# Values unit of an attention kernel: query tiles outside, the two key tiles inside

## The chip, the cores and the metric

One core of a Trainium2 chip runs the kernel. The metric is the device time of one execution in microseconds (us). The executions of each kernel agree within 0.2%, with a granted TensorE clock of 0.999 or 1.0. The clock is the one granted to TensorE, the matrix engine, as a share of full speed.

## The reference, cut to what matters

The reference normalises `x` (2048 rows of 640), runs attention with 32 heads of width 192 over caches of 2048 keys, multiplies the result by a gated feed-forward branch and adds `x`. The change touches one product only, the probabilities times the values:

```python
H, Dh = 32, 192
scores = jnp.einsum("bhqd,bhkd->bhqk", q, k_cache) * (Dh ** -0.5)
p = _softmax(scores, axis=-1)
o = jnp.einsum("bhqk,bhkd->bhqd", p, v_cache)          # this product
return o.transpose(0, 2, 1, 3).reshape(B, Sq, H * Dh) @ wo
```

## The kernel before

For each head, each block of 512 queries and each pair `p` of key tiles (two tiles of 128 keys), TensorE computes scores into PSUM (the memory that takes its results), ScalarE takes the exponential into `pT2` (128 keys on the partitions; columns 0 to 511 are the 512 queries for key tile 0, columns 512 to 1023 for key tile 1), and TensorE multiplies `pT2` with V. That last part is the *values unit*. There are 32 heads x 4 query blocks x 8 pairs = 1024 units.

V lies in `vt`: 16 rows (one per key tile) of 192 values, a column of ones for the softmax sum, and one column of padding, so 194 bf16 numbers or 388 bytes a row.

```python
vts = [vtp.tile([P, NKT, DH + 2], BF16, name=f"vt{i}") for i in range(2)]
# ... cut: loads of K, V and weights, LayerNorm, projections ...
def emit_scores(h, qb, p):
    # ... cut: operands
    for r, (ka, qa, kb, qb2) in enumerate(rounds):          # 3 rounds of 2 row halves, 512 columns
        nc.tensor.matmul(st2[:, 0:512], lhsT=ka, rhs=qa, start=r == 0 and nr == 3, stop=r == nr - 1)
        nc.tensor.matmul(st2[:, 512:1024], lhsT=kb, rhs=qb2, start=r == 0 and nr == 3, stop=r == nr - 1)
    pT2 = pp.tile([P, 1024], BF16, tag="pT2", name="pT2")
    nc.scalar.activation(out=pT2[:], in_=st2[:], func=ACT.Exp, scale=att_scale)
    return pT2

def values(n):
    # ... cut: PSUM tiles obanks[0], obanks[1] at p == 0
    vt = loads[h]["vt"]
    pT2 = exps.pop(n)
    for t in range(2):                                      # key tile
        for j in range(4):                                  # query tile
            start = p == 0 and t == 0 and j % 2 == 0
            stop = p == NPAIR - 1 and t == 1 and j % 2 == 1
            for r in range(2):                              # row half of the array
                nc.tensor.matmul(obanks[r][:, j * 256:j * 256 + DH + 1],
                                 lhsT=pT2[r * 64:(r + 1) * 64, t * 512 + j * P:t * 512 + (j + 1) * P],
                                 rhs=vt[r * 64:(r + 1) * 64, 2 * p + t, 0:DH + 1], start=start, stop=stop)
    # ... cut: after the last pair VectorE adds the two halves and divides by the sums
```

The stationary operand (`lhsT`) is a 64 x 128 piece of `pT2`; the moving operand (`rhs`) is half of a V row tile, 64 partitions by 193 columns. The two matmuls of the inner loop use the two row halves of the array and run side by side (in the trace of before the second starts 3 ns after the first, in the median); I call them a *pair of matmuls*, so a unit is eight pairs in a row.

## Time and profile before

| | before |
|---|---|
| time, median of 6 runs | 1941.95 us (1940.68 to 1942.10) |
| PE busy in the profiled run | 1929.6 of 1938.7 us |
| share of values matmuls in the chain of waits | 35% |
| PE waiting for other engines | 3.5 us in all |

The first view is the page of the profiled run: span, busy time of each engine, the chain of waits by engine and by line, then groups of instructions (line, engine, operation, output<-inputs, shapes, count | busy us, mean ns of one | idle time of the engine before them).

```profile
span 1938.7 us, 59672 instructions
...
PE 1929.6 (100%) x27273; PEld 1318.5 (68%) x27281; DVE 654.0 (34%) x997; ACT 1180.2 (61%) x1278; POOL 282.6 (15%) x501
...
PE 98%; DVE 1%; DMA 0%; ACT 0%; issue 0%; POOL 0%; DVEq 0%; ACTq 0%
PE obank L516 35%; PE st L487 33%; PE ps L424 14%; PE ps_s L111 11%; PE ps_f L727 3%; PE ps_gu L701 1%; PE st L488 1%; DVE stats L316 0%; PE ps L410 0%; DMA x_all<-in_A_x_dram 0%; DVE xn L346 0%; PE ps L391 0%; PE pst L354 0%; DVE mv L317 0%; PE pk L271 0%
...
L516 PEld LDWEIGHTS <-pT 64*128 64x128 bf16 x16384 | 713.7, 94 | 242.2 <-ACT pT L490 0.2
L516 PE MATMUL obank<-vt,pT 64*128 64x193 bf16 x16384 | 851.8, 243 | 0.0
L487 PE MATMUL st<-qC,KW 64*128 64x512 bf16 x2046 | 605.6, 376 | 0.1
...
```

PE, the matmul engine, is never out of work, and 98% of the chain is PE. The Trainium skill, "Trainium Kernel Development and Optimization", section "Performance Expectations", calls matmul busy time a bad metric for how close a kernel is to roofline, because matmuls are pipelined. The trace agrees that busy time hides the pace: 16384 values matmuls of 243 ns would be 3981 us; they are busy for 851.8 us together because they overlap. So the spacing of their starts has to be read, not their length.

The second view lists what PE waited for (us in total, times, longest).

```profile
...
engine line waited for: us in total, times, longest us
PE pk L569 <- POOL ident_bf masks.py:199: 2.8, 1, 2.8
PE st L487 <- ACT pT L490: 0.3, 1, 0.3
PE pst L354 <- DVE xn L346: 0.2, 1, 0.2
PE st L483 <- DVE qA L393: 0.2, 1, 0.2
```

After the start nothing makes PE wait. The third view follows V's tile: the instructions that read or write it (shortest, median and longest ns, first and last start in us), and who waited for it.

```profile
...
engine op xcount: duration ns min/median/max, first and last start us, forms
L516 PE MATMUL obank<-vt,pT x16384: 241/243/253, 16.0 to 1646.4; 64*128 64x193 bf16 x200
...
  DVE osum L525: 788.9, 127
...
DMA to landing us min/median/max: 3.6/5.6/7.5
```

The last values matmul starts at 1646.4 us; the remaining 292 us are the other stages.

From the start times of the single matmuls in the trace I worked out the distance from the start of each pair of matmuls to the next, averaged over the units of the trace that are complete and hold no wait (1016 of 1024; a unit with a distance over 120 ns is left out). The last column is the time of the three pairs of scores just ahead of a unit, averaged over all 1022 such stretches:

```
           pair:   1     2     3     4     5     6     7     8    unit  | 3 pairs of scores
before           83.3  83.3  83.3  83.3  87.5  82.5  82.5  82.8  668.6 | 647.5 ns
```

The fifth pair stands out. It is the one at which the moving operand goes from the even V row (key tile 0) to the odd one (key tile 1).

One more line, of the view of groups kept apart by shape: 48 full-array matmuls that accumulate onto one PSUM address back to back.

```profile
...
L111 PE MATMUL ps_s<-wo_sb,oT 128*128 128x128 bf16 x48 | 2.8, 219 | 0.0
...
```

### The profile page before, as it was taken

How to read it: one execution, taken by the hardware profiler on the slowest of the kernel's cores; microseconds unless marked ns; L12 is line 12 of the kernel's file. 1: busy time of each engine (PE TensorE's matmuls, PEld its weight loads, DVE VectorE, ACT ScalarE, POOL GpSimd, SP SyncE). 2: the span in 40 equal slices, each digit the busy share in tenths (PEclk: the TensorE clock that was granted, in tenths of full speed). 3: DMA queues.
4: the chain of work that ended last, by engine and by line, in shares of the span. 5: the costliest groups of instructions: out<-in, count | busy, mean ns of one | idle time of the engine just before them, and what ended most of it. 6: DMA issues, size and time to landing. Idle time of an engine off the chain costs nothing.

```text
span 1938.7 us, 59672 instructions
## 1 busy us (share of the span) xinstructions
PE 1929.6 (100%) x27273; PEld 1318.5 (68%) x27281; DVE 654.0 (34%) x997; ACT 1180.2 (61%) x1278; POOL 282.6 (15%) x501
## 2 busy tenths in 40 slices
PE   9999999999999999999999999999999999999998
PEld 6666666666666666666666666666666666577776
DVE  7333333333333333333333333333333334521111
ACT  6677676767676767776767777677767677210000
POOL 3111111111111111111111111111111110000000
PEclk9999999999999999999999999999999999999999
DMA  7643433323233433353434333434333220937772
GB/s 181 129 101 67 98 68 86 83 60 88 59 89 62 99 62 98 68 162 68 101 65 100 68 101 68 101 64 100 69 71 94 57 69 2 262 67 135 152 152 61
DMA packets 394643, 178.98 MB, mean 92 GB/s; under 512 B 341616, under 2 KB 382832, under 8 KB 394384
## 3 DMA queue, kind: packets, MB, share of 16 engines
q1 hardware_dynamic: 371136, 125.32, 30.3%
q0 software_dynamic: 19472, 45.71, 9.6%
q8 instruction: 215, 3.52, 0.8%
q10 hardware_dynamic: 3776, 4.06, 0.6%
q14 instruction: 44, 0.36, 0.1%
HBM read 52.82 MB, written 27.79 MB: 42 GB/s over the span
## 4 chain that ended last, share of the span: by engine, by line
PE 98%; DVE 1%; DMA 0%; ACT 0%; issue 0%; POOL 0%; DVEq 0%; ACTq 0%
PE obank L516 35%; PE st L487 33%; PE ps L424 14%; PE ps_s L111 11%; PE ps_f L727 3%; PE ps_gu L701 1%; PE st L488 1%; DVE stats L316 0%; PE ps L410 0%; DMA x_all<-in_A_x_dram 0%; DVE xn L346 0%; PE ps L391 0%; PE pst L354 0%; DVE mv L317 0%; PE pk L271 0%
## 5 line engine op out<-in xcount | busy, mean ns | idle before, releaser
L490 ACT ACTIVATE pT<-st 128x1024 bf16<-128x1024 f32 x1024 | 1046.2, 1022 | 251.8 <-PE st L488 236.2
L516 PEld LDWEIGHTS <-pT 64*128 64x128 bf16 x16384 | 713.7, 94 | 242.2 <-ACT pT L490 0.2
L516 PE MATMUL obank<-vt,pT 64*128 64x193 bf16 x16384 | 851.8, 243 | 0.0
L487 PE MATMUL st<-qC,KW 64*128 64x512 bf16 x2046 | 605.6, 376 | 0.1
L525 DVE COPY osum<-obank 128x772 f32<-128x772 f32 x128 | 123.0, 961 | 788.9 <-PE obank L516 788.9
L488 PE MATMUL st<-qB,KW 64*128 64x512 bf16 x1024 | 385.0, 376 | 0.0
L487 PE MATMUL st<-qA,KW 64*128 64x512 bf16 x1022 | 384.3, 376 | 0.4 <-ACT pT L490 0.3
L488 PE MATMUL st<-qC,KW 64*128 64x512 bf16 x1022 | 384.3, 376 | 0.0
L488 PE MATMUL st<-qA,KW 64*128 64x512 bf16 x1022 | 384.3, 376 | 0.0
L487 PEld LDWEIGHTS <-KW 64*128 64x128 bf16 x3068 | 278.0, 94 | 153.8 <-issue 2.1
L424 PE MATMUL ps<-xnT,W 64*128 64x512 bf16 x1280 | 297.2, 376 | 0.0
L424 PE MATMUL ps<-xnS,W 64*128 64x512 bf16 x1280 | 296.3, 376 | 0.0
L488 PEld LDWEIGHTS <-KW 64*128 64x128 bf16 x3068 | 278.0, 94 | 0.7 <-issue 0.6
L377 POOL DMA_DIRECT2D qC<-qA x124 | 65.4, 528 | 1285.6 <-DVE rl_all L532 1270.0
L430 ACT CAST qB<-ps 128x512 bf16<-128x512 f32 x131 | 76.7, 586 | 228.5 <-PE ps L424 222.9
L111 PE MATMUL ps_s<-wo_sb,oT 128*128 128x384 bf16 (+3 forms) x1535 | 208.8, 299 | 0.1
L424 PEld LDWEIGHTS <-W 64*128 64x128 bf16 x2560 | 122.9, 94 | 121.2
L111 PEld LDWEIGHTS <-oT 128*128 128x128 bf16 x1536 | 148.4, 98 | 60.4
L526 DVE TENSOR_TENSOR osum<-osum,obank 128x772 f32<-128x772 f32 x128 | 122.7, 958 | 13.4
L533 DVE TENSOR_TENSOR ostage<-osum,rl_all 128x768 bf16<-128x768 f32 x128 | 122.6, 958 | 4.4
L465 DVE SCALAR_TENSOR_TENSOR hT<-pt,qB 64x512 bf16<-64x512 bf16 x64 | 43.8, 684 | 199.5 <-ACT pt L464 199.5
L429 DVE CAST qA<-ps 128x512 bf16<-128x512 f32 x131 | 90.5, 691 | 25.2 <-PE ps L410 7.3
(84 smaller groups left out, 623.8 us busy)
## 6 DMA issues: line engine op xcount, KB each, us to landing
o_scr<-ostage SPq DMA_DIRECT2D x16, 1536.0 KB, 10.0
vt<-in_A_v_cache_dram SPq DMA_DIRECT2D x63, 384.0 KB, 5.6
qC<-qA POOLq DMA_DIRECT2D x248, 64.0 KB, 1.9
qC<-qB POOLq DMA_DIRECT2D x124, 64.0 KB, 2.3
wo_sb<-in_A_wo_dram POOLq DMA_DIRECT2D x1, 7680.0 KB, 35.3
W<-in_A_wq_dram POOLq DMA_DIRECT2D x32, 160.0 KB, 3.4
W<-in_B_w_dram POOLq DMA_DIRECT2D x32, 80.0 KB, 3.1
W<-in_A_wq_dram POOLq DMA_DIRECT2D x32, 80.0 KB, 2.9
```

The lines of the kernel that those rows point to most:

```text
L111: nc.tensor.matmul(ps[:, 0:w], lhsT=oT[:, k, :], rhs=wo_sb[:, k, c0:c1], start=(k == 0), stop=(k == OC - 1))
L377: nc.gpsimd.dma_start(out=qC[0:64, half, :], in_=qAB[half][64:P, :])
L424: nc.tensor.matmul(ps[:, r * 512:(r + 1) * 512], lhsT=W[rows, j, :], rhs=xs[rows, j // 2, qs], start=(j == 0), stop=(j == 2 * DC - 1))
L429: a = nc.vector.tensor_copy(out=qAB[0][:], in_=ps[:, 0:512])
L430: b = nc.scalar.copy(out=qAB[1][:], in_=ps[:, 512:1024])
L487: nc.tensor.matmul(st2[:, 0:512], lhsT=ka, rhs=qa, start=r == 0 and nr == 3, stop=r == nr - 1)
L488: nc.tensor.matmul(st2[:, 512:1024], lhsT=kb, rhs=qb2, start=r == 0 and nr == 3, stop=r == nr - 1)
L490: nc.scalar.activation(out=pT2[:], in_=st2[:], func=ACT.Exp, scale=att_scale)
L516: nc.tensor.matmul(obanks[r][:, j * 256:j * 256 + DH + 1], lhsT=pT2[r * 64:(r + 1) * 64, t * 512 + j * P:t * 512 + (j + 1) * P], rhs=vt[r ...
L525: nc.vector.tensor_copy(out=osum[:], in_=ov[0])
L526: nc.vector.tensor_tensor(out=osum[:], in0=osum[:], in1=ov[1], op=ALU.add)
L533: nc.vector.tensor_tensor(out=ostage[:, qb * 4:qb * 4 + 4, hg * DH:(hg + 1) * DH], in0=osum[:, :, 0:DH], in1=rl.unsqueeze(2).to_broadcast( ...
```

## The change

The intent was to finish one query tile (both key tiles) before going to the next. The same 16 matmuls run, in another order.

```diff
         pT2 = exps.pop(n)
-        for t in range(2):
-            for j in range(4):
+        for j in range(4):
+            for t in range(2):
                 start = p == 0 and t == 0 and j % 2 == 0
                 stop = p == NPAIR - 1 and t == 1 and j % 2 == 1
                 for r in range(2):
```

The accumulation stays right: each `start` flag is still on the first matmul into its half of the tile, and e2, which has the same order, passed the comparison with the reference.

## The prediction

> **What bounds it.** TensorE. The page gives PE busy for 1929.6 of 1938.7 us at a granted clock of 0.99 or more, the chain of waits is 98% PE, and in the table of waits PE waits for other engines for 3.5 us in all. So any time the change adds to or takes from TensorE's stream is the change in the kernel's time; ACT (61%) and DVE (34%) have slack.
>
> **What the values unit costs.** The values matmuls are 35% of the chain: 1024 units of 16 matmuls, run as 8 pairs (both row halves of the array at once). From the trace's start times, averaged over 1021 complete units, a unit takes 669.5 ns; its pairs' start-to-start times are 83.3, 83.3, 83.3, 83.3, 87.5, 82.5, 82.5, 82.8 ns. The Trainium skill, "TensorE: Matmul & The Clock Gate", section "Back-to-back issue gap", gives N/2.4 + 2.5, so 82.9 ns for 193 columns: the trace agrees but for the fifth pair, which costs 4.6 ns more in every unit.
>
> **What the change does.** It permutes the 16 matmuls of a unit. Count, shapes, weight loads, PSUM groups and the other engines' instruction order stay. What moves:
> 1. Each PSUM address is written again one pair (83 ns) after its first write, not four pairs (333 ns).
> 2. The V operand changes row at each pair; before, once, at the fifth pair.
> 3. In the first unit of each head the wait for V's second half comes at the third matmul instead of the ninth, 0.25 us sooner. V was loaded a head earlier: no cost.
>
> **Costing.** (1) I expect 0: in the last output tile 48 matmuls of 128 columns accumulate onto one address back to back, 56 ns apart, at the normal rate. (2) is where the fifth pair matters. Rows of V are 194 bf16 = 388 bytes, so even rows start at a multiple of 8 bytes and odd rows 4 bytes off. Scores and projections change their moving operand at each pair too, between well-aligned tiles, and show no extra (215.8 ns for 512 columns). So I read the fifth pair as the cost of going from an aligned to a misaligned row. (The Trainium skill, "SBUF — State Buffer", Specifications, speaks of lines of 16 bytes; no run here shows that as the mechanism.) Going back seems free: the scores after a unit start on time. After the change a unit has four such steps instead of one: three more at 5 ns, 15 ns per unit, x 1024 = 15 us, all on the critical path. If going back costs the same, six more: 28 us (1970). If the fifth pair's extra comes from something else (returning to the first PSUM bank, say), it may vanish (1938) or stay (1942).
>
> **Prediction.** 1955 us, 0.7% slower; 8 in 10 within 1938 to 1970. Faster by over 2%: 0.01. Within 2%: 0.93. Slower by over 2%: 0.06.
>
> **What would show it.** PE still about 100% busy and 98% of the chain; the values line's share up by under one point; scores and projections unchanged; within a unit the second, fourth, sixth and eighth pairs at about 87.5 ns, the others near 83 (right), or all at 83 (step (2) wrong), or both directions at 87; no new wait on V or PSUM.
>
> **What would make it wrong.** A stall when two row halves accumulate onto one address 83 ns apart, which no part of this trace tests (the 56 ns case used the full array): even 20 ns on four pairs would be 82 us. Or a different cost of switching back to an aligned row within a unit.

Two notes on it. Its unit of 669.5 ns averages 1021 units, some of which hold a wait; the 1016 without one give 668.6 ns. Its 82.9 ns is an estimate from the page's formula, which the page gives for a single isolated matmul, not for a stream with weight loads. The undisturbed pairs of this trace take 83.3 ns.

## The result

| | before | after |
|---|---|---|
| time, median of 6 runs each | 1941.95 us | 1947.25 us (1946.97 to 1948.81) |
| ratio of the fast runs | 1 | 1.003, 95% interval 1.0017 to 1.0043 |
| span of the profiled run | 1938.7 us | 1945.2 us |
| values unit, eight pairs | 668.6 ns | 676.8 ns |
| three pairs of scores | 647.5 ns | 645.6 ns |

A ratio here is always the mean time of one kernel's fast runs over that of the other's in the same rounds, so it is not quite the ratio of the medians. The change costs 5.3 us by the medians and 6.5 us between the two profiled runs. The predicted 1955 us has the right sign and is too large: 13 us were forecast and 5.3 came. 1947.25 lies inside the stated range of 1938 to 1970.

The page of after, the same lines as above:

```profile
span 1945.2 us, 59672 instructions
...
PE 1935.1 (99%) x27273; PEld 1323.2 (68%) x27281; DVE 654.4 (34%) x997; ACT 1180.2 (61%) x1278; POOL 282.6 (15%) x501
...
PE 98%; DMA 1%; DVE 1%; ACT 0%; SPq 0%; issue 0%; DVEq 0%; ACTq 0%
PE obank L516 35%; PE st L487 33%; PE ps L424 14%; PE ps_s L111 11%; PE ps_f L727 3%; PE ps_gu L701 1%; DMA x_all<-in_A_x_dram 1%; PE st L488 1%; PE ps L410 0%; DVE stats L316 0%; ACT KW L277 0%; PE pst L354 0%; ACT xnT L356 0%; SPq L289 0%; DVE qA L429 0%
...
L516 PEld LDWEIGHTS <-pT 64*128 64x128 bf16 x16384 | 717.7, 94 | 242.3 <-ACT pT L490 0.2
L516 PE MATMUL obank<-vt,pT 64*128 64x193 bf16 x16384 | 857.7, 243 | 0.0
L487 PE MATMUL st<-qC,KW 64*128 64x512 bf16 x2046 | 604.4, 375 | 0.1
...
```

PE is still the only bound. The values group is 5.9 us busier (857.7 against 851.8), with the same count and the same 243 ns each. (Busy time counts to the modelled end of the last matmul, so what delays the start of the scores behind it is not all in it.)

PE's waits after:

```profile
...
engine line waited for: us in total, times, longest us
PE pk L569 <- POOL ident_bf masks.py:199: 2.8, 1, 2.8
PE pst L354 <- DVE xn L346: 0.7, 1, 0.7
PE pst L354 <- DVE qA L429: 0.7, 1, 0.7
PE st L487 <- ACT pT L490: 0.3, 1, 0.3
PE st L483 <- DVE qA L393: 0.2, 1, 0.2
```

The waits are 1.2 us longer, all in the kernel's first 24 us and in lines that the change does not touch: 0.5 us before the first scores, and 0.7 us in one wait of the transposes at 23.6 us. The first values matmul still starts at 16.0 us in both, so only the second wait falls inside the attention stage. Nothing waits on V or on a PSUM bank in either kernel. V's tile after:

```profile
...
engine op xcount: duration ns min/median/max, first and last start us, forms
L516 PE MATMUL obank<-vt,pT x16384: 240/243/253, 16.0 to 1653.0; 64*128 64x193 bf16 x200
...
  DVE osum L525: 793.8, 127
...
DMA to landing us min/median/max: 3.9/5.5/7.9
```

The last values matmul starts 6.6 us later than before (1653.0 against 1646.4), and behind it follow 292 us as before. The lost time therefore lies in the attention stage, and the starts of its pairs show where:

```
           pair:   1     2     3     4     5     6     7     8    unit  | 3 pairs of scores
before           83.3  83.3  83.3  83.3  87.5  82.5  82.5  82.8  668.6 | 647.5 ns
after            83.3  87.5  82.5  86.2  82.5  86.1  82.5  86.1  676.8 | 645.6 ns
```

As predicted, the extra sits at the second, fourth, sixth and eighth pair, the four steps from the even to the odd V row. But only the first costs as much as the fifth did before; the pair behind each one runs at 82.5 ns, not 83.3, and the scores are 1.9 ns shorter. By these means the net is 8.2 - 1.9 = 6.3 ns per unit. That is a little too much, because some of the scores averaged here follow projections and not a unit. The plainest measure is the mean distance from the start of one unit to the start of the next, where only three pairs of scores lie between them (888 stretches in each trace): 1316.2 ns before, 1322.0 ns after, so 5.9 ns more, times 1024 = 6.0 us.

The difference of the two spans, 6.5 us, agrees with this once the wait at 23.6 us is taken out. Between the first and the last values matmul after takes 6.5 us more: by my sum of all start-to-start distances, values 8.2 us more, scores 2.0 us and projections 0.3 us less, and waits 0.6 us more. So the change itself costs 5.9 us in this pair of traces.

What remained to be found out: what makes the step expensive (alignment, as I had predicted, or something else), and why three more steps cost about 6 ns and not 15.

### The profile page after: what moved, and what is told of

The parts are those of the page before. It is cut to its first block, busy times and chain, and to the rows that moved or that the text cites. A ratio compares the mean times of both kernels' runs of the same rounds, so it can differ in the third digit from the quotient of the medians.

```text
span 1945.2 us, 59672 instructions
## 1 busy us (share of the span) xinstructions
PE 1935.1 (99%) x27273; PEld 1323.2 (68%) x27281; DVE 654.4 (34%) x997; ACT 1180.2 (61%) x1278; POOL 282.6 (15%) x501
## 4 chain that ended last, share of the span: by engine, by line
PE 98%; DMA 1%; DVE 1%; ACT 0%; SPq 0%; issue 0%; DVEq 0%; ACTq 0%
PE obank L516 35%; PE st L487 33%; PE ps L424 14%; PE ps_s L111 11%; PE ps_f L727 3%; PE ps_gu L701 1%; DMA x_all<-in_A_x_dram 1%; PE st L488 1%; PE ps L410 0%; DVE stats L316 0%; ACT KW L277 0%; PE pst L354 0%; ACT xnT L356 0%; SPq L289 0%; DVE qA L429 0%
## 5 line engine op out<-in xcount | busy, mean ns | idle before, releaser
L516 PE MATMUL obank<-vt,pT 64*128 64x193 bf16 x16384 | 857.7, 243 | 0.0
```

The lines of the kernel that those rows point to most:

```text
L516: nc.tensor.matmul(obanks[r][:, j * 256:j * 256 + DH + 1], lhsT=pT2[r * 64:(r + 1) * 64, t * 512 + j * P:t * 512 + (j + 1) * P], rhs=vt[r ...
```

## The experiments

All 18 ran five rounds, each beside the kernel before on the same chip; the groups of runs ran on different chips, so the ratios are the surer comparison between groups. All passed the comparison with the reference; for e5 and e6, which compute a wrong product, this shows only that the comparison's tolerance does not see it. Each edit is shown or told against the kernel named; the moves of loads and of the column of ones that go with it are left out. Every table of pair starts is made as above. Expectations are quoted as they stood before the runs; their theories A, B, C, then M, S, then N, G, then "offset rule" and "seam theory" replaced each other as they fell.

### First round: alignment to 8 bytes, row change, or PSUM

**e1_before_pad4**, before with

```diff
-vtp.tile([P, NKT, DH + 2], ...
+vtp.tile([P, NKT, DH + 4], ...
```

> The order of before, V rows padded from 388 to 392 bytes, so that every row starts at a multiple of 8 bytes. Theory A (a step from a row aligned to 8 bytes to one 4 bytes off costs TensorE 4 to 5 ns): the fifth pair falls from 87.5 to about 83 ns, the unit from 669.5 to about 665, the time by 4 to 5 us to about 1937.5. Theory B (a step to the other V row costs, whatever its alignment) and theory C (PSUM: coming back to an address just written costs): fifth pair stays at 87.5, time 1942.

Measured: 1940.71 us (before 1941.36), ratio 0.9997 (0.9984 to 1.0011). The fifth pair stays at 87.5 ns, the unit at 668.6.

**e2_after_pad4**, the same edit on after.

> The order of after, V rows padded to 392 bytes. Theory A: all eight pairs at about 83 ns, time the same as e1_before_pad4 within 1 us, about 1937.5, so the change's 5.3 us vanish. Theory B: pairs 2, 4, 6, 8 keep about 86 to 87.5 ns, time 1947. Theory C: the same as B, 1947, because the PSUM order is that of after.

Measured: 1946.81 us, ratio 1.0027 (1.0013 to 1.0040); pairs 83.3, 87.5, 82.5, 86.1, 82.5, 86.1, 82.5, 86.1: the same as after. The values group in the page of e2, to be set beside after's 857.7:

```profile
...
L516 PE MATMUL obank<-vt,pT 64*128 64x193 bf16 x16384 | 857.4, 243 | 0.0
...
```

Every row now starts at a multiple of 8 bytes, and nothing changed. My theory A, the reason given in the prediction, is dead.

**e3_serpentine**, before with

```diff
-        for t in range(2):
-            for j in range(4):
+        for j in range(4):
+            for u in range(2):
+                t = u if j % 2 == 0 else 1 - u
```

(and `u` for `t` in the `start` and `stop` flags)

> V rows unpadded (388 bytes), query tiles outside as in after, but the key tile order turned round in every other query tile: 0 1, 1 0, 0 1, 1 0. PSUM addresses are written again after one pair just as in after. Theory A: only pairs 2 and 6 step from an aligned to a misaligned row, so they show about 87, the others 82 to 83; unit about 673, time about 1944.5 (half way between before and after). Theory B: row changes at pairs 2, 4, 6, 8, four extras, 1947. Theory C: second writes at pairs 2, 4, 6, 8, four extras, 1947.

Measured: 1943.34 us, ratio 1.0012 (0.9999 to 1.0026).

```
           pair:   1     2     3     4     5     6     7     8    unit  | scores
key tile           0     1     1     0     0     1     1     0
e3               83.3  87.5  82.5  82.6  82.7  87.5  82.5  82.6  671.2 | 647.0 ns
```

```profile
...
L517 PE MATMUL obank<-vt,pT 64*128 64x193 bf16 x16384 | 854.1, 243 | 0.0
...
```

The group's 854.1 us lie between before and after. Pairs 4 and 8 write a PSUM address again after one pair, as pairs 2 and 6 do, and cost nothing: theory C (PSUM) falls. Pairs 4 and 8 also change the V row, from odd to even, for free: theory B (any change of row) falls as well. Only the step from tile 0 to tile 1 costs. (The time came near theory A's number, 1944.5, though e2 had refuted that theory.)

**e4_all_off4**, before with rows of 392 bytes and V from element 2 on in each row (loads, ones and `rhs` moved by two elements).

> The order of before, V rows padded to 392 bytes but V starting 4 bytes into each row, so that all rows are 4 bytes off a multiple of 8. Theory A: the step to a misaligned row now comes once per unit, from the scores to the first pair: first pair about 87.5, fifth pair about 82.5, time within 2 us of before (1942). Theory B and C: fifth pair stays at 87.5, first at 83.

Measured: 1941.45 us, ratio 1.0000 (0.9986 to 1.0014); fifth pair still 87.5 ns, first 83.3. Against theory A again.

### Second round: moving or stationary operand, and distance

A step from tile 0 to tile 1 changes both operands. e5 and e6 keep one of them.

**e5_same_row**, after with

```diff
-rhs=vt[r * 64:(r + 1) * 64, 2 * p + t, 0:DH + 1]
+rhs=vt[r * 64:(r + 1) * 64, 2 * p, 0:DH + 1]
```

> The order of after, but both key tiles multiply the even V row (wrong result on purpose): the moving operand no longer changes inside a unit, the stationary operand still alternates between the halves of pT2. Theory M (the step from the even to the odd V row, the moving operand, costs): all pairs 83.3 or less, unit about 664 to 667, time about 1937 to 1940. Theory S (the step from the first to the second half of pT2, the stationary operand, costs): pairs 2, 4, 6, 8 stay at 86 to 87.5, time 1947.

Measured: 1939.20 us (before 1941.48), ratio 0.9988 (0.9975 to 1.0002); all pairs 83.3 to 83.4 ns, unit 666.7.

**e6_same_weights**, after with

```diff
-lhsT=pT2[..., t * 512 + j * P:t * 512 + (j + 1) * P]
+lhsT=pT2[..., j * P:(j + 1) * P]
```

> The order of after, but both key tiles use the first half of pT2 as stationary operand (wrong result on purpose), the V row still alternates. Theory M: pairs 2, 4, 6, 8 stay at 86 to 87.5, time 1947. Theory S: all pairs at 83.3 or less, time about 1937 to 1940.

Measured: 1947.16 us, ratio 1.0029 (1.0015 to 1.0043); the eight pairs as in after. The values group of e5, then of e6:

```profile
...
L516 PE MATMUL obank<-vt,pT 64*128 64x193 bf16 x16384 | 849.5, 243 | 0.0
...
```

```profile
...
L516 PE MATMUL obank<-vt,pT 64*128 64x193 bf16 x16384 | 857.7, 243 | 0.0
...
```

849.5 against 857.7 us: the whole cost belongs to the moving operand, theory M. PSUM sees the same addresses in both.

**e7_before_odd_first**, before with `for t in (1, 0):` (and the flags turned to match).

> The order of before with the odd key tile first, then the even one, in each unit. The serpentine run showed an extra only at steps from tile 0 to tile 1, so both theories M and S: no extra at the fifth pair; the unit is 2 to 5 ns shorter and the time 2 to 4 us less than before (1938 to 1940), unless the step from the scores to tile 1 costs the same at the first pair, then 1941.5.

Measured: 1940.05 us (1938.72 to 1940.49), ratio 0.9990 (0.9977 to 1.0004); all eight pairs 83.3, unit 666.7, scores 647.5 ns.

```profile
...
L516 PE MATMUL obank<-vt,pT 64*128 64x193 bf16 x16384 | 849.6, 243 | 0.0
...
```

So before's own single step costs 668.6 - 666.7 = 1.9 ns per unit, not the 4.6 ns that the prediction counted for its fifth pair: the three pairs behind it win most of it back.

**e8_after_pad64**, after with rows of 512 bytes (`DH + 64`).

> The order of after with V rows padded to 512 bytes, so that the odd row no longer starts just behind the end of the even row (128 bytes lie between) and all rows start at a multiple of 512 bytes. Theory M with adjacency or any finer alignment than 8 bytes as its reason: extras vanish, time about 1940 or less. Theory S, or M for any step whatever the distance: pairs 2, 4, 6, 8 stay at 86 to 87.5, time 1947.

Measured: 1939.01 us, ratio 0.9990 (0.9976 to 1.0003); all eight pairs 83.3, unit 666.7.

```profile
...
L516 PE MATMUL obank<-vt,pT 64*128 64x193 bf16 x16384 | 849.5, 243 | 0.0
...
```

The order of after, without any extra. The loop order by itself is not the cause; how the V rows lie is.

### Third round: near, or aligned to more than 8 bytes

**e9_tiles_apart**, after with the rows of key tile 0 and of key tile 1 in two blocks (`rhs` row `t * NPAIR + p` instead of `2 * p + t`, loads to match).

> The order of after, row length 388 bytes as in after, but the rows of key tile 0 and of key tile 1 lie in two blocks, so the odd row starts 3104 bytes behind the even one, not 388. Theory N (what costs is that the odd row starts just behind the end of the even one): all pairs 83.3, time 1939. Theory G (what costs is a start that is not at a multiple of some block larger than 8 bytes): rows are aligned no better than in after, so extras remain in most units, time 1944 to 1947.

Measured: 1939.12 us (before 1941.23), ratio 0.9988 (0.9974 to 1.0001); all pairs 83.3.

```profile
...
L517 PE MATMUL obank<-vt,pT 64*128 64x193 bf16 x16384 | 849.5, 243 | 0.0
...
```

**e10_after_pad8**, after with rows of 400 bytes (`DH + 8`).

> The order of after, V rows of 400 bytes: all rows start at a multiple of 16 bytes and 14 bytes lie between the end of the even row and the start of the odd one. Theory G with blocks of 16 bytes: no extras, 1939. Theory N with a reach of under 14 bytes: the same, no extras. Theory N with a reach of more, or G with larger blocks: pairs 2, 4, 6, 8 at 86 to 87.5, 1947. (392 bytes, 6 bytes between, still had the extras.)

Measured: 1939.25 us, ratio 0.9988 (0.9975 to 1.0002); all pairs 83.3.

**e11_after_pad32**, after with rows of 448 bytes (`DH + 32`).

> The order of after, V rows of 448 bytes: rows start at multiples of 64 bytes, 62 bytes lie between. With e10 it brackets the size: whichever of the two still shows the extras (pairs 2, 4, 6, 8 at 86 to 87.5, time 1947) tells how far the effect reaches; between 14 and 62 bytes if only e10 has them, between 62 and 126 if both have.

Measured: 1938.61 us, ratio 0.9989 (0.9976 to 1.0003); all pairs 83.3.

**e12_gap2_stride512**, after with rows 512 bytes apart and the even rows at byte 124 of theirs.

> The order of after, rows 512 bytes apart as in e8 (which had no extras), but the even rows moved to the end of their 512 bytes, so that 2 bytes lie between the even row's end and the odd row's start, as in after; odd rows start at multiples of 512 bytes. Theory N: extras back at pairs 2, 4, 6, 8 (86 to 87.5), time 1947. Theory G (alignment of the odd row's start): no extras, time 1939.

Measured: 1942.17 us, ratio 1.0003 (0.9989 to 1.0017).

```
           pair:   1     2     3     4     5     6     7     8    unit  | scores
e12              83.3  83.3  86.7  82.5  85.0  82.5  85.0  82.5  670.8 | 646.1 ns
```

```profile
...
L520 PE MATMUL obank<-vt,pT 64*128 64x193 bf16 x16384 | 852.7, 242 | 0.0
...
```

Neither theory foretold this. Only 2 bytes lie between the rows, and the odd row starts 388 bytes behind the even one, both as in after; yet the step from even to odd is free. So neither nearness counted in bytes nor the distance from row to row is the reason. But the step *back* now costs, from the odd row at byte 0 of a 16-byte line to the even row at byte 12 of one. Together with e9 (even and odd row always at the same place within 16 bytes) and e10 (both at its start) this suggested a rule about the place within 16 bytes.

### Fourth round: the place within 16 bytes

I had two rules. The offset rule: a step to a larger offset within a 16-byte line costs. The seam theory: the last line of one row and the first of the next, both used in part, cost when together they hold fewer than about 8 or 9 elements (in before 1 + 6 or 5 + 2).

**e13_before_pad8**, before with rows of 400 bytes, the control to e10.

> Control: the order of before with V rows of 400 bytes. If the loop order costs nothing by itself and only the rows' offsets within 16 bytes do: all pairs 83.3, unit 666.7, time 1939, the same as e10_after_pad8 within 1 us. If the order also costs or gains something by itself: a difference to e10 of over 1 us.

Measured: 1939.13 us (before 1941.36), ratio 0.9987 (0.9973 to 1.0000); all pairs 83.3, unit 666.7. With e10's 1939.25 us: once the rows lie apart, the two orders take the same time.

```profile
...
L516 PE MATMUL obank<-vt,pT 64*128 64x193 bf16 x16384 | 849.6, 243 | 0.0
...
```

**e14_even8_odd0**, after with rows of 400 bytes and the even rows moved by 8 bytes.

> The order of after, rows of 400 bytes, but the even rows start 8 bytes into a 16-byte line and the odd rows at its start. Both theories: no extra at the pairs of the odd row, extras of 3 to 4 ns at pairs 3, 5, 7 (steps from offset 0 to offset 8), as with e12; time about 1942 to 1944.

Measured: 1939.23 us, ratio 0.9989 (0.9975 to 1.0002), shorter than expected. Pairs 83.3, 83.3, 85.8, 82.5, 82.5, 82.5, 85.8, 82.5, unit 668.3, scores 646.1 ns. Only two of the three steps back show an extra, and the pairs and scores behind them win it back.

**e15_198_columns** and **e16_195_columns**, after with rows of 416 bytes, odd rows moved by 4 bytes, and 198 or 195 columns in place of 193:

```diff
+V0 = (0, 2)      # first element of even and odd rows
+NV = 195         # e15: 198
-vtp.tile([P, NKT, DH + 2], ...
+vtp.tile([P, NKT, DH + 16], ...
-    rhs=vt[..., 2 * p + t, 0:DH + 1]        # out: j * 256:j * 256 + DH + 1
+    rhs=vt[..., 2 * p + t, V0[t]:V0[t] + NV]  # out: j * 256:j * 256 + NV
```

> The order of after, even rows at offset 0 and odd rows at offset 4 of a 16-byte line as in the first half of the rows of after, but 198 columns are multiplied, not 193 (the five more are ones and are not read), so the even row's last line holds 6 elements, not 1. [...]Offset rule (any step to a larger offset costs): alternating pairs, 85 and 88 to 89 ns, time about 1960. Seam theory (last and first line together hold 6 + 6 = 12 elements, which is enough): all pairs 85.0, time about 1953.

> As e15 but with 195 columns: the even row's last line holds 3 elements, the odd row's first 6, so 9 together, as many as at a seam of two aligned rows of 193 columns, which showed no extra. Offset rule: alternating pairs, 84.2 and 87 to 88 ns, time about 1954. Seam theory: all pairs at 84.2 ns, time about 1946, shorter than with the offset rule although two columns more are multiplied than in after.

Measured: e15 1952.92 us (ratio 1.0058, 1.0044 to 1.0072), all pairs 85.0; e16 1945.80 us (1.0023, 1.0009 to 1.0036), all pairs 84.2. Both are what the seam theory foretold, to 0.2 us. (The five extra columns of e15 took 1.7 ns per pair, 85.0 against 83.3.) It looked settled; but these two had changed the row length as well as the number of columns, so the control was run.

**e18_193_columns**, the same with 193 columns.

> The layout of e15 and e16 (rows of 416 bytes, even rows at offset 0, odd rows at offset 4 of a 16-byte line) with 193 columns, seams of 1 + 6 = 7 elements from even to odd. Seam theory and offset rule: as in after, pairs 2, 4, 6, 8 at 86 to 87.5, unit 676 to 677, time 1947, longer than e16 with its 195 columns. If the layout and not the columns had freed e15 and e16: 83.3 throughout, 1939.

Measured: 1938.61 us (before 1941.53), ratio 0.9985 (0.9972 to 0.9999).

```
           pair:   1     2     3     4     5     6     7     8    unit  | scores
e18              83.3  85.0  82.5  82.5  83.3  85.0  82.5  82.5  666.7 | 647.5 ns
```

```profile
...
L521 PE MATMUL obank<-vt,pT 64*128 64x193 bf16 x16384 | 850.0, 243 | 0.0
...
```

**e17_194_columns**, the same with 194 columns.

> The same with 194 columns: seams of 2 + 6 = 8 elements, exactly one line's worth. If a full line's worth is enough: all pairs 83.3 to 83.8, time about 1939 to 1942. If more than one line's worth is needed: extras as in after, time 1944 to 1948.

Measured: 1938.58 us, ratio 0.9986 (0.9972 to 0.9999); the same eight distances as e18, unit 666.7.

The control failed, and with it both rules: the seam holds 1 + 6 elements and the step goes from offset 0 to offset 4, as in after, but the unit loses nothing: the 1.7 ns more at pairs 2 and 6 are won back by the pairs behind them. The layout, rows of 416 bytes with the odd ones moved by 4, is free with 193 columns too, so e15 and e16 had not needed their extra columns. Kept as they stood, those two successes would have been a false proof.

### What survives

Set e18 beside the units of after with an even `p`. Both step from offset 0 to offset 4, with 193 columns; the odd row starts 388 bytes behind the even one in after and 420 in e18. The first costs 10.1 ns per unit (676.8 - 666.7, the same for even and odd `p`), the second nothing. In after the even row's 386 bytes end inside a 16-byte line, and the odd row starts in that *same* line. The tile starts at a multiple of 64 bytes in the built program, so this can be counted for each kernel (e12 and e14 are told of below the table; e15 and e16 multiply more columns and are left out):

| kernels | odd row starts in the line where the even row ended | steps even to odd per unit | time |
|---|---|---|---|
| e7 (odd row first) | yes | 0 | 1940.05 us |
| e5 (odd row unused) | - | 0 | 1939.20 us |
| e8, e9, e10, e11, e18 and, with 194 columns, e17 (order of after) | no | 4 | 1938.58 to 1939.25 us |
| e13 (order of before) | no | 1 | 1939.13 us |
| before, e1, e4 | yes | 1 | 1940.71 to 1941.95 us |
| e3 | yes | 2 | 1943.34 us |
| after, e2, e6 | yes | 4 | 1946.81 to 1947.25 us |

In this table the kernel takes 1938.6 to 1940.1 us in either order without a shared line, or without a step across it; with it, each step adds about 2 us over the 1024 units: 1, 2 and 4 steps stand at about +2, +4 and +8 us. The distance from unit to unit says the same with less noise: 1314.2 ns in e7 to e11 and e13, and 2.0 ns more in before (one step), 4.0 in e3 (two) and 7.9 in after (four). If sharing is the reason, the block that matters is larger than 8 bytes: in e1 and e2 the even row ends 386 and the odd row starts 392 bytes behind the start of the even one, in different blocks of 8 bytes, and the cost is still there. It is no larger than 16 bytes: in e10 the even row ends and the odd row starts in the same 32 bytes but in different 16-byte lines, at no cost. The Trainium skill, "SBUF — State Buffer", section "Specifications", gives the lines of SBUF, the memory in which V lies, as "16-byte (need ≥2 hits per line for full bandwidth; each cross to a new line pays a penalty)". The size agrees with these runs; the page says nothing of a stream that begins in the line where the one before it ended. That it is the re-use of the line which stalls the array's input was argued from this table; it is not shown. No run shows the inside of it, and none changed the sharing of the line alone with all else equal: e18 also puts every odd row 32 bytes farther from its even row, and e12, which keeps the distance, moves both rows' places within their lines and pays at the step back.

Open stays a second, smaller effect: e12 and e14 share no line, yet lose 4.1 and 1.6 ns per unit in their values at steps back to a row that starts late in its line. From unit to unit e14 has won it all back (0.1 ns left), as e18 has, but e12 keeps 2.6 ns, and its 1942.17 us. So a shared line is not the only layout that costs. One rule for both effects was not found.

## Why the prediction was wrong, point by point

- *TensorE bounds the kernel; a change of its stream is the change of the time.* Right. PE is 98% of the chain in both, and its stream accounts for 5.9 of the 6.5 us between the two spans; the rest is the wait at 23.6 us.
- *(1) Writing a PSUM address again after 83 ns costs 0.* Right. e10 and e13 differ in nothing but the order and take 1939.25 and 1939.13 us (ratios to before 0.9988 and 0.9987); e3 and e5 say the same.
- *(3) The earlier wait for V's second half costs nothing.* Right: no wait on V in the waits of after.
- *The extra belongs to the step to the odd V row, and going back is free.* Right for this layout, shown by e5, e6, e3 and e7; in e12 and e14 going back does show an extra. The four steps stand where they were expected, but only the first reached the 87.5 ns foretold; the others took 86.1 or 86.2.
- *The reason is that odd rows are 4 bytes off a multiple of 8.* Wrong. With 8-byte alignment nothing changes (e1, e2); with a step to a row 4 bytes off but farther away the loss is gone (e18). The extra still came at the foretold pairs, because the rows that are 4 bytes off are also those that start in a shared line: there the wrong reason and the measured pattern fell together by luck.
- *"Three more at 5 ns, 15 ns per unit, x 1024 = 15 us".* This is the step that failed. The term was mis-sized: a step costs about 2 ns net, not 5. I took the excess of the fifth pair over the page's figure, 87.5 - 82.9 = 4.6 ns, rounded up, as the cost. But the pairs behind it ran *faster* than undisturbed, at 82.5 ns: in the kernels without an extra every pair takes 83.3 ns, so before's step costs 668.6 - 666.7 = 1.9 ns. Each further step was 86.1 or 86.2 against a following 82.5, and the scores won back about 2 ns more; the prediction had expected the scores unchanged. Three steps at 2 ns x 1024 make 6 us, 1948, against 1947.25 measured. Recovery behind a slow pair is what the costing left out. The number could have been read from the trace of before: the unit's sum, 668.6, less eight times the undisturbed 83.3, is 2 ns.

## What to carry to other kernels

When a stream of short operations shows a slow one, cost it by the sum over the whole repeating stretch against an undisturbed stretch, not by its distance from its neighbours, which may be catching up. In this kernel it paid to lay the rows that TensorE streams one after the other so that they share no 16-byte line (not proof that sharing is the reason): eight columns of padding in place of two (e13, one line) brought before from about 1941.4 to 1939.1 us and made the two loop orders equal (e10), a gain of 0.1% at the edge of what five rounds can tell. And run the control even when a forecast is met to 0.2 us: e15 and e16 fitted a theory that e18 refuted.

## What the Trainium skill lacked or had wrong

- "SBUF — State Buffer", Specifications, lacks any word on a moving operand which starts in the 16-byte line where the previous one ended. In the runs with such steps each costs about 2 ns net (from unit to unit 2.0 ns for one step in before, 7.9 ns for four in after); that the shared line is the reason is argued, not shown.
- "TensorE: Matmul & The Clock Gate", Back-to-back issue gap: the formula N/2.4 + 2.5, which the page gives for an isolated matmul, yields as estimates 82.9 ns for 193 columns and 83.75 for 195; measured for pairs in a stream were 83.3 and 84.2, its values for 194 and 196. With 194, 198 and 512 columns it meets the runs (83.3, 85.0 and 215.8 ns). The page lacks that an odd count costs as much as the next even one, as the two odd counts run here do.
- None of the pages used here explains the extras of e12 and e14 (4.1 and 1.6 ns per unit in the values), or that the pairs behind a stall run at 82.5 ns, 0.8 ns below the undisturbed 83.3.
